# An attention and two-MLP kernel on one core: the first block's output matmul in plain fp32, and the short block moved to the end

## The chip, the core and the metric

One core of a Trainium2 chip. The metric is the device time of one launch in microseconds (us). Engines: PE (matrix multiply; PEld is its weight load), DVE (vector), ACT (scalar, activation functions), POOL (GpSimd), SP (issues the DMAs here).

## The reference, cut to what matters

With `q`, `k`, `v` of 6016 tokens x 256 channels:

```
qn, kn = q / (norm over tokens + 1e-6), k / (norm over tokens + 1e-6)
x  = v @ softmax(kn.T @ qn / tau)                     # 256 x 256 attention over channels
h  = x @ w_in                                         # 6016 x 2048
g  = (a0 + a1 h + a2 h^2 + a3 h^3) / (1 + |b0| |h| + |b1| h^2 + 1e-6)
x2 = g @ w_out                                        # 6016 x 256      (MLP 1)
h  = x2 @ w_in2
g  = h * clip(h + 3, 0, 6) / 6
out = g @ w_out2                                      # 6016 x 256      (MLP 2)
```

The four weights come as float64 (4 MB each) and are turned into fp32 on the chip, a quarter ("group" 0 to 3, 1 MB) at a time.

## The kernel before, in words

**Stages.** First q and k stream in, in 14 chunks of 1, 2, ten times 4, 3 and 1 rows per partition. PE multiplies them in fp32 (L250), ACT squares them (L240), DVE adds the squares (L242). Then come the norms (L281 to L304), the softmax (L319 to L327), and `w1` = attention times `w_in` (`W0a` ... `W3`, L339), so that MLP 1 is `v @ w1`. Its result is split into a high and a low part (`E..h` on ACT, `E..l` on DVE, L349 and L351).

**Split matmuls.** A plain fp32 matmul takes several passes in the array. So the MLP's operands are split: high part (fp32r) and low part (the rest, fp32r). A product is then high x high, low x high (weights) and high x low: 6 passes for each of two output halves, 12 fp32r matmuls with N = tokens of the block. One such set of 12 is called an M below.

**Blocks and steps.** `BLOCKS = [384] + [512] * 11` tokens. A step does 256 of the 2048 hidden channels of a block, so a block has 8 steps and there are 96, with MLP 2 running 10 steps behind MLP 1. In a step s: `M1` (input matmul, L374), `U1` = |b1 h| and `P1` on ACT; `DS`, `P2`, `P3` on DVE; `AB`, `LN`, `EX` on ACT, which make 1/Q as exp(-ln Q). For step s-1: `HI` (high part of g), `N2` and `DD` on DVE, `LO` (low part of g) on DVE or, as `LOP`, on POOL. `M3` is the output matmul of step s-2 (L379, into `y`). MLP 2: `M2` (L374), `C1` (ACT), `C2` (DVE), `H2` (ACT), `L2` or `L2P` (DVE or POOL), `M4` (L379, into `o`). `Vh`, `Vl`, `Yh`, `Yl` split the inputs of the MLPs.

**Weight conversion.** `conv(name, group, part)`: `s` and `b` on ACT, `j` on DVE (the fp32 weight), `h` on ACT (its high part), `l` on DVE or `p` on POOL (its low part).

**Order.** Each engine runs its queue in order. For steps 0 to 21 the order of all engines is the hand-made list `FILL`; after that `ORDER` repeats per step. `chain` ties the instructions of each engine to that order. `shares` remembers the last DVE instruction that reads two SBUF tiles, and `behind` makes a POOL instruction wait for it.

**Tiles.** Working tiles of 128 x 1024 fp32 come from pools by tag: `U` 3, `P` 3, `B` 2, `C` 2, `hi` 3, `lo` 3, `vo` 1. The q and k chunks use `hi`, `U`, `lo`, `P`, so a chunk's load waits until an earlier chunk is done with its tile.

Of the kernel before, what the change touches and what calls it, by code (L numbers as in the profile page):

```python
# [18 lines left out]
BLOCKS = [384] + [512] * 11  # L19
# [42 lines left out]
def attention_rational_relu6_kernel(ctx: ExitStack, tc, q, k, vT, tau, w_in, w_out, ca, cb, w_in2, w_out2, outT):  # L62
# [139 lines left out]

# [56 lines left out]
    nc.sync.dma_start(out=col[:, 0:4], in_=ca.partition_broadcast(128))
    load_w("wi1", 1)
    load_v(0)
    load_w("wi1", 2)
    load_w("wi1", 3)
    for name in ("wo1", "wi2"):  # L270
        for g in range(4):
            load_w(name, g)
# [3 lines left out]
    nc.vector.reciprocal(out=rt, in_=TAU)
    s2k, s2q = tails
    for i in range(4):
        a, t = ((acc_k, s2k), (acc_q, s2q))[i // 2]
        h = slice((i % 2) * 128, (i % 2) * 128 + 128)  # L280
        nc.tensor.matmul(ssp[:, 0, i:i + 1], a[:, h], ones[:, 0:1], start=True, stop=False)  # L281
        nc.tensor.matmul(ssp[:, 0, i:i + 1], t[:, h], ones[:, 0:1], start=False, stop=True)
# [16 lines left out]
    for c in range(2):
        nc.vector.tensor_scalar(out=diag[:, c * 128:(c + 1) * 128], in0=ident, scalar1=inv[:, 2 + c:3 + c], scalar2=None, op0=ALU.mult)  # L300

    nc.vector.tensor_scalar(out=inv[:, 0:2], in0=inv[:, 0:2], scalar1=rt, scalar2=-1.0, op0=ALU.mult, op1=ALU.mult)
    products(LAST - 1)
    nc.tensor.matmul(ssp[:, 1, 0:256], ones, diag, start=True, stop=True)  # L304
    products(LAST)
    for p in "sbj":
        conv("wi1", 1, p)
    split_v(0, "h")
    split_v(0, "l")
# [326 lines left out]
```

## Time and profile before

| | |
|---|---|
| time, 3 runs | 1145.67 us median (1145.56 to 1145.82) |
| span of the profiled execution (first to last instruction) | 1141.5 us; its time around the span is not recorded, the median lies 4.2 us above it |
| PE busy | 1100.4 us, 96% |
| DVE busy | 1009.6 us, 88% |
| ACT busy | 819.8 us, 72% |
| POOL busy | 251.6 us, 22% |

```profile
PE   8986689999999999999999999999999999999998
DVE  6689999988999999998998998998998999999954
ACT  6798986776776777777677676786776776776643
PEclk9998899999999999999999999999999999999999
DMA  9980000000010010010010010010010010000000
```

Each digit is a slice of 28.5 us, in tenths of its length; PEclk is the granted TensorE clock in tenths of full speed.

### The profile page before, as it was taken

What the parts mean: (1) busy time and instruction counts of PE and PEld (TensorE: products, weight loads), DVE (VectorE), ACT (ScalarE), POOL (GpSimd) and SP (SyncE); (2) the same over time, 40 slices, a digit from 0 to 9 for tenths busy, and PEclk for the clock granted to TensorE, in tenths of its full rate; (3) what the DMA queues carried; (4) which work ended last, traced back from release to release, by engine and by line L of the source; (5) the groups of instructions that cost most, each with busy time, mean ns of one, the idle gap of its engine ahead of it and who ended that gap; (6) DMA issues with size and microseconds to landing.
All of it is one profiled execution on the core that took longest, in us unless ns stands there. A gap on an engine that the chain in (4) does not pass through costs nothing.

```text
span 1141.5 us, 12312 instructions
## 1 busy us (share of the span) xinstructions
PE 1100.4 (96%) x4870; PEld 914.1 (80%) x4870; DVE 1009.6 (88%) x872; ACT 819.8 (72%) x802; POOL 251.6 (22%) x115
## 2 busy tenths in 40 slices
PE   8986689999999999999999999999999999999998
PEld 7756578877888888888888888888888888888887
DVE  6689999988999999998998998998998999999954
ACT  6798986776776777777677676786776776776643
POOL 0013335222221222212212222122122221221200
PEclk9998899999999999999999999999999999999999
DMA  9980000000010010010010010010010010000000
GB/s 358 369 327 1 19 1 1 15 19 1 1 37 1 1 38 1 1 37 1 1 37 1 1 38 1 1 37 1 1 37 1 1 37 1 1 19 1 1 19 18
DMA packets 17464, 42.20 MB, mean 37 GB/s; under 512 B 1536, under 2 KB 2560, under 8 KB 17408
## 3 DMA queue, kind: packets, MB, share of 16 engines
q1 hardware_dynamic: 17408, 41.43, 9.9%
q8 instruction: 38, 0.62, 0.2%
q14 instruction: 18, 0.15, 0.0%
HBM read 35.26 MB, written 6.16 MB: 36 GB/s over the span
## 4 chain that ended last, share of the span: by engine, by line
PE 86%; DVE 6%; ACT 4%; issue 2%; DMA 1%; POOL 0%; SPq 0%; POOLq 0%; DVEq 0%; ACTq 0%
PE h L374 41%; PE y L379 21%; PE o L379 20%; PE y L250 3%; DVE B L421 1%; ACT P L406 1%; DVE P L430 1%; DVE P L416 1%; ACT U L411 1%; DVE hi L544 1%; DVE P L556 1%; DMA lo<-in_q_dram 1%; DVE B L550 1%; ACT U L434 0%; DVE q L160 0%
## 5 line engine op out<-in xcount | busy, mean ns | idle before, releaser
L485 POOL TENSOR_TENSOR lo<-C,hi 128x1024 fp32r<-128x1024 f32 (+1 forms) x82 | 195.4, 2383 | 680.5 <-DVE lo L561 649.6
L411 ACT ACTIVATE U<-h,col 128x1024 f32<-128x1024 f32 (+1 forms) x96 | 105.7, 1101 | 180.2 <-PE h L374 179.6
L374 PE MATMUL h<-vh,w 128*128 128x512 f32 (+1 forms) x768 | 194.7, 397 | 20.0 <-DVE P L430 18.8
L379 PE MATMUL y<-hi,wo 128*128 128x512 f32 (+1 forms) x800 | 198.7, 385 | 0.4 <-DVE hi L544 0.4
L374 PEld LDWEIGHTS h<-vh,w 128*128 128x128 f32 x768 | 147.9, 195 | 52.7 <-issue 21.5
L374 PE MATMUL h<-yh,wi 128*128 128x512 f32 (+1 forms) x768 | 187.1, 385 | 3.0 <-DVE C L474 1.8
L379 PE MATMUL o<-hi,wo 128*128 128x512 f32 (+1 forms) x736 | 182.6, 384 | 0.0
L421 DVE SCALAR_TENSOR_TENSOR B<-U,aB,h 128x1024 f32<-128x1024 f32 (+1 forms) x96 | 120.6, 1256 | 61.8 <-ACT P L406 61.6
L379 PEld LDWEIGHTS y<-hi,wo 128*128 128x128 f32 x800 | 149.3, 188 | 29.2 <-DVE hi L544 0.7
L374 PEld LDWEIGHTS h<-yh,wi 128*128 128x128 f32 x768 | 143.2, 188 | 32.3 <-DVE C L474 3.2
L379 PEld LDWEIGHTS o<-hi,wo 128*128 128x128 f32 x736 | 137.6, 188 | 26.6
L469 ACT ACTIVATE C<-h,imm 128x1024 f32<-128x1024 f32 (+1 forms) x96 | 105.1, 1095 | 62.6 <-PE h L374 60.0
L474 DVE SCALAR_TENSOR_TENSOR C<-C,h 128x1024 f32<-128x1024 f32 (+1 forms) x96 | 114.0, 1187 | 16.1 <-ACT C L469 16.1
L544 DVE SCALAR_TENSOR_TENSOR hi<-P,col,U 128x1024 fp32r<-128x1024 f32 (+1 forms) x96 | 125.3, 1306 | 1.0 <-ACT U L438 0.9
L430 DVE SCALAR_TENSOR_TENSOR P<-P,col,h 128x1024 f32<-128x1024 f32 (+1 forms) x96 | 120.7, 1257 | 3.9 <-ACT U L411 1.2
L556 DVE SCALAR_TENSOR_TENSOR P<-P,col,B 128x1024 f32<-128x1024 f32 (+1 forms) x96 | 121.0, 1261 | 2.7
L406 ACT ACTIVATE P<-h,col 128x1024 f32<-128x1024 f32 (+1 forms) x96 | 113.3, 1181 | 6.9 <-PE h L374 5.1
L550 DVE SCALAR_TENSOR_TENSOR B<-B,hi 128x1024 f32<-128x1024 f32 (+1 forms) x96 | 115.8, 1207 | 2.7
L416 DVE TENSOR_TENSOR P<-P,h 128x1024 f32<-128x1024 f32 (+1 forms) x96 | 114.5, 1193 | 3.4 <-ACT U L411 1.9
L480 ACT ACTIVATE hi<-C 128x1024 fp32r<-128x1024 f32 (+1 forms) x96 | 99.6, 1037 | 23.8 <-DVE C L474 21.8
L379 PE MATMUL y<-lo,wo 128*128 128x512 f32 (+1 forms) x400 | 108.3, 388 | 7.6 <-POOL lo L561 7.6
L434 ACT ACTIVATE U<-B,imm 128x1024 f32<-128x1024 f32 (+1 forms) x96 | 108.9, 1134 | 2.7
(101 smaller groups left out, 1296.6 us busy)
## 6 DMA issues: line engine op xcount, KB each, us to landing
raw_wi<-in_moe_w_in_dram SPq DMA_DIRECT2D x8, 1024.0 KB, 13.4
raw_wo<-in_moe_w_out_dram SPq DMA_DIRECT2D x8, 1024.0 KB, 15.1
vo<-in_v_dram SPq DMA_DIRECT2D x11, 512.0 KB, 3.7
out_dram<-vo SPq DMA_DIRECT2D x10, 512.0 KB, 2.8
hi<-in_k_dram SPq DMA_DIRECT2D x5, 512.0 KB, 9.4
lo<-in_q_dram SPq DMA_DIRECT2D x5, 512.0 KB, 10.2
U<-in_k_dram SPq DMA_DIRECT2D x5, 512.0 KB, 10.1
P<-in_q_dram SPq DMA_DIRECT2D x5, 512.0 KB, 10.2
```

The lines of the kernel that those rows point to most:

```text
L374: nc.tensor.matmul(h[j], w_in_at(name, a, c, f + j), x[b][:, c, :], start=(i == 0), stop=(i == 5))
L379: nc.tensor.matmul(y[d], w_out_at(name, a, 2 * pr + j, d), g[b][j], start=(pr == 0 and i == 0), stop=(pr == 7 and i == 5))
L406: nc.scalar.activation(out=halves(c["P"], T), in_=c["h"], func=AF.Identity, scale=A3, bias=A2)
L411: nc.scalar.activation(out=halves(c["U"], T), in_=c["h"], func=AF.Abs, scale=B1)
L416: nc.vector.tensor_tensor(out=p, in0=p, in1=c["h"], op=ALU.mult)
L421: nc.vector.scalar_tensor_tensor(out=halves(c["B"], T), in0=halves(c["U"], T), scalar=aB0, in1=c["h"], op0=ALU.add, op1=ALU.mult)
L430: nc.vector.scalar_tensor_tensor(out=p, in0=p, scalar=A1, in1=c["h"], op0=ALU.add, op1=ALU.mult)
L474: nc.vector.scalar_tensor_tensor(out=x, in0=x, scalar=6.0, in1=h, op0=ALU.min, op1=ALU.mult)
L485: i2 = e.tensor_tensor(out=x, in0=y, in1=z.bitcast(F32), op=ALU.subtract)
L544: shares(nc.vector.scalar_tensor_tensor(out=c["Hi"][:, fa], in0=P[:, fa], scalar=A0, in1=U[:, fa], op0=ALU.add, op1=ALU.mult))
L550: shares(nc.vector.scalar_tensor_tensor(out=B[:, fa], in0=B[:, fa], scalar=ONE_EPS, in1=c["Hi"][:, fa].bitcast(F32), op0=ALU.add, op1=ALU. ...
L556: shares(nc.vector.scalar_tensor_tensor(out=P[:, fa], in0=P[:, fa], scalar=A0, in1=B[:, fa], op0=ALU.add, op1=ALU.subtract))
```

## The change

- `BLOCKS` becomes `[512] * 11 + [384]`.
- For steps 0 to 7 of MLP 1 (now a block of 512 tokens) g is kept as one fp32 tile. `m_out` then does 4 fp32 matmuls with the unsplit fp32 weight (`single`) in place of 12 fp32r ones. `LO` is gone in these steps. P is made with negated coefficients, and `DD` becomes `hi = (B - 2) * hi`.
- In the same steps the denominator comes from r = |h| sqrt|b1|: `U1` uses sqrt|b1|, `DS` is `(U + |b0| / sqrt|b1|) * U` (U only, no longer `h`), `AB` adds the constant 1 + 1e-6, `LN` has no bias, and `N2` is a plain product `B * U` that no longer reads `HI`'s result. It may run on POOL (`N2P`). The small values for that are made once (`nB`, `nN`, `nR`, `nS`, `nQ`).
- The fp32 weight of `wo1` lies in a `lo` tile until its group's `h` and `p` parts and the first block's `M3` are done.
- `LOP` now goes through `behind`; the tiles of `LO`, `L2`, `Vl`, `Yl` are allocated where they are written.
- The list now also orders the q and k phase, with a load item for each DMA (`lk`, `lq`, `lw`, `lv`, `ls`); one group of `w_in2` is loaded and converted (`s`, `b`, `j`, `h`) among the q and k chunks.

```
-BLOCKS = [384] + [512] * 11
+BLOCKS = [512] * 11 + [384]
+F3 = R1 = QX = frozenset(range(8))        # F2, F4 are empty
...
     def m_out(y, name, g, pr, T, split=False):
+        if len(g) == 1:
+            for j, d in ((j, d) for j in range(2) for d in range(2)):
+                o = 256 * ((2 * pr + j) % 4) + 128 * d
+                nc.tensor.matmul(y[d], single[name, pr // 2][:, o:o + 128], g[0][j],
+                                 start=(pr == 0 and j == 0), stop=(pr == 7 and j == 1))
+            return
...
             def DS():
+                if s in R1:
+                    shares(nc.vector.scalar_tensor_tensor(out=c["B"][:, f], in0=c["U"][:, f], scalar=CB, in1=c["U"][:, f],
+                                                          op0=ALU.add, op1=ALU.mult))
+                    return
...
+            def n2(e):
+                U, B, P = operands()
+                x = U[:, fa] if one else c["Hi"][:, fa].bitcast(F32)
+                if a in QX:
+                    i = e.tensor_tensor(out=B[:, fa], in0=B[:, fa], in1=x, op=ALU.mult)
...
+                (shares if e is nc.vector or a not in QX else behind)(i)
...
+                if one:
+                    hi = c["Hi"][:, fa]
+                    shares(nc.vector.scalar_tensor_tensor(out=hi, in0=B[:, fa], scalar=2.0, in1=hi, op0=ALU.subtract, op1=ALU.mult))
+                    hl1[a] = [halves(c["Hi"], Ta)]
...
+            elif name == "wo1" and F3:
+                f = wk.tile([128, 1024], I32, tag="lo", name="f", bufs=BUFS["lo"])
```

Two pieces of the new list, from the q and k phase and from the norms and softmax:

```
lk0 lq1 lq0 lq2 lk1 lk2 ... lk13 ... lq3 ... lk3 ... lk4 ... lq4 ... lk5 x2 lk6 ... lq5 ... lwi22 lq6 lq9 ... lq7 ... lk7 ... lq8 x5 lq12
nM wi1:0s n0 lv0 x12 nN n1 n2 wi1:0b wo1:2b lwi13 nD wi1:0j nC x13 lwo11 zm0 zm1 Vh ze0 zt0 ze1 wo1:2s zc0 zt1 nQ wi2:2p zc1 wi1:3b W0a
```

What the two lists hold between the starts of M1 (wide: 1024 elements per partition, 512 tokens; narrow: 768 elements, 384 tokens; `w1` evictions: `E` items of 512 and of 256 columns; fp32: `M3` of the first block, or a `W` item):

| from, to | list | DVE wide + conversion | DVE narrow | DVE evictions | PE sets wide, narrow, fp32 | POOL | ACT |
|---|---|---|---|---|---|---|---|
| M1@0, M1@4 | before | 0 + 2 | 19 | 5, 2 | 0, 6, 2 | 3 | 33 |
| | after | 15 + 4 | 0 | 6, 2 | 4, 0, 3 | 3 | 26 |
| M1@4, M1@10 | before | 6 + 9 | 30 | 0 | 2, 9, 0 | 7 | 46 |
| | after | 28 + 1 | 0 | 0 | 6, 0, 5 | 4 | 32 |
| M1@10, M1@16 | before | 43 + 4 | 11 | 0 | 12, 14, 0 | 11 | 56 |
| | after | 56 + 6 | 0 | 0 | 23, 0, 2 | 14 | 68 |
| M1@16, M1@21 | before | 37 + 0 | 2 | 0 | 16, 3, 0 | 6 | 35 |
| | after | 37 + 1 | 0 | 0 | 20, 0, 0 | 10 | 36 |

After `M1@21` itself the list of before holds no further M, that of after one (`M4@20`); otherwise both end with the same sets done.

## Rows read from the trace of the kernel before

**Rows 1.** Busy time by engine, clock and DMA, in stretches of 50 us
```profile
core 0: us, PE busy (x) PEld busy (x) DVE busy (x) ACT busy (x) POOL busy (x), PEclk, DMA share, GB/s
0.00:50.00 50.00, 47.12 (x218) 40.93 (x218) 35.29 (x43) 32.97 (x39) 2.70 (x11) 1.00 0.95 360
...
100.00:150.00 50.00, 33.52 (x140) 29.47 (x140) 49.05 (x47) 47.11 (x50) 19.65 (x9) 0.84 0.04 11
...
500.00:550.00 50.00, 50.00 (x223) 41.40 (x222) 44.46 (x38) 35.30 (x33) 12.04 (x5) 1.00 0.07 22
```

**Rows 2.** The same view between the starts of M1@0, @4, @10, @16, @21 and the end
```profile
59.88:89.02 29.14, 21.33 (x90) 15.70 (x89) 23.78 (x29) 26.84 (x34) 6.03 (x3) 0.99 0.74 282
89.02:136.34 47.32, 31.10 (x133) 28.28 (x133) 45.25 (x46) 43.41 (x48) 15.51 (x7) 0.82 0.04 11
136.34:207.00 70.66, 65.83 (x313) 57.08 (x313) 67.53 (x59) 56.95 (x58) 28.43 (x12) 0.98 0.00 1
207.00:259.80 52.80, 50.79 (x228) 42.11 (x229) 47.55 (x40) 34.68 (x35) 13.37 (x6) 1.00 0.05 18
259.80:1141.50 881.70, 876.77 (x3864) 725.12 (x3864) 783.41 (x646) 616.62 (x581) 185.56 (x77) 1.00 0.04 12
```

**Rows 3.** PE's waits, 0 to 180 us: total us, times, longest
```profile
PE h L374 <- DVE P L430: 16.2, 5, 7.3
PE y L379 <- POOL lo L561: 7.4, 3, 4.2
```

**Rows 4.** Timeline of PE: start us, us, instruction
```profile
30.57 3.62 PE L250 MATMUL y<-lo,hi 128*128 128x256 f32 x16
34.02 3.62 PE L250 MATMUL y<-P,U 128*128 128x256 f32 x16
...
71.96 3.60 PE L339 MATMUL o<-raw_wi,hi 128*128 128x512 f32 x8
...
174.57 1.55 PE L379 MATMUL o<-hi,wo 128*128 128x384 f32 x8
...
176.65 2.01 PE L374 MATMUL h<-vh,w 128*128 128x512 f32 x8
...
1053.37 1.98 PE L374 MATMUL h<-vh,w 128*128 128x512 f32 x8
...
1056.09 1.98 PE L374 MATMUL h<-yh,wi 128*128 128x512 f32 x8
```

**Rows 5.** Timeline of DVE: first row of a gapless run, and the one after it
```profile
84.89 1.01 DVE L556 SCALAR_TENSOR_TENSOR P<-P,col,B 128x768 f32<-128x768 f32 x1
...
87.67 0.74 DVE L351 SCALAR_TENSOR_TENSOR w<-o,small,w 128x512 fp32r<-128x512 f32 x1
...
188.25 1.28 DVE L544 SCALAR_TENSOR_TENSOR hi<-P,col,U 128x1024 fp32r<-128x1024 f32 x1
...
196.54 0.94 DVE L474 SCALAR_TENSOR_TENSOR C<-C,h 128x768 f32<-128x768 f32 x1
```

**Rows 6.** Timeline of DVE, norms and softmax (in brackets: idle before, and its releaser)
```profile
42.81 0.16 DVE L289 TENSOR_SCALAR small<-o 128x4 f32<-128x4 f32 x1
...
50.32 0.48 DVE L319 SCALAR_TENSOR_TENSOR yl<-y,small,yh 128x256 f32<-128x256 f32 x1 [2.60 <-ACT yh L310]
...
53.51 0.42 DVE L325 COPY hi<-h 128x256 f32<-128x256 f32 x1 [0.59 <-PE h L324]
```

**Rows 7.** Busy time, clock and DMA of 30 to 40 us (columns of Rows 1)
```profile
30.00:40.00 10.00, 10.00 (x48) 8.81 (x47) 9.56 (x12) 7.16 (x9) 0.00 (x0) 1.00 0.87 316
```

**Rows 8.** Timeline of POOL and DVE, side by side
```profile
137.48 1.84 POOL L561 TENSOR_TENSOR lo<-P,U 128x768 fp32r<-128x768 f32 x1
137.49 2.92 DVE L544 SCALAR_TENSOR_TENSOR hi<-P,col,U 128x1024 fp32r<-128x1024 f32 x1
```

**Rows 9.** Groups by form, 59.88 to 259.8 us: count, busy us, mean ns, idle before
```profile
L544 DVE SCALAR_TENSOR_TENSOR hi<-P,col,U 128x1024 fp32r<-128x1024 f32 x12 | 18.7, 1561 | 1.0 <-ACT U L438 0.9
...
L171 POOL TENSOR_TENSOR wi<-q,wi 128x1024 fp32r<-128x1024 f32 x4 | 9.6, 2397 | 5.0 <-ACT P L406 5.0
```

More of the change, by code (lines that the diff above doesn't have):

```diff
@@ L31 @@
 FILL = (
[23 rows of a table removed]
[27 rows of a table added]
 )
 ONE_EPS = 1.0 + 1e-6
+F3 = frozenset(range(8))
+F4 = frozenset()
+F2 = frozenset()
+R1 = frozenset(range(8))
+QX = frozenset(range(8))
 ET = mybir.EngineType
@@ L265, in attention_rational_relu6_kernel @@
[L265 to L272, printed above, removed]
-    rt = small[:, 0:1]
[L276 to L282, printed above, removed]
@@ L283, in attention_rational_relu6_kernel @@
-    for p in "sbj":
-        conv("wi1", 0, p)
-    products(NORM_AT + 1)
+        parts_done.append(i)
+    rt = small[:, 0:1]
     aB0 = const.tile([128, 1], F32, name="aB0")
-    nc.scalar.activation(out=aB0, in_=B0, func=AF.Abs)
+    neg = const.tile([128, 4], F32, name="neg")
+    rbc = const.tile([128, 4], F32, name="rbc")
+    N0, N1, N2_, N3 = (neg[:, i:i + 1] for i in range(4))
+    RB, CB = rbc[:, 0:1], rbc[:, 1:2]
     ss, ln, y0, iy, nrm, inv = (small[:, 4 * j:4 * j + 4] for j in range(1, 7))
-    nc.vector.tensor_scalar(out=ss, in0=ssp[:, 0, 0:4], scalar1=1e-30, scalar2=None, op0=ALU.max)
@@ L299, in attention_rational_relu6_kernel @@
[L299 to L309, printed above, removed]
-    nc.scalar.activation(out=qb, in_=ssp[:, 1, 0:256], func=AF.Copy)
@@ new lines, in softmax @@
+    def softmax(part, c):
+        h, sc = half[c], late["sc"]
+        if part == "m":
+            nc.vector.scalar_tensor_tensor(out=sc[:, h], in0=sp[:, c, 0:256], scalar=inv[:, c:c + 1], in1=late["qb"], op0=ALU.mult, op1=ALU.mult)
+            nc.vector.tensor_reduce(out=nmax[:, c:c + 1], in_=sc[:, h], axis=AX.X, op=ALU.min)
+        elif part == "e":
+            nc.scalar.activation(out=sc[:, h], in_=sc[:, h], func=AF.Exp, scale=-1.0, bias=nmax[:, c:c + 1], accum_out=sm[:, c:c + 1])
+        elif part == "t":
+            if not ep:
+                ep.append(ptile("h1"))
+            for d in range(2):
+                nc.tensor.transpose(ep[0][:, c, d * 128:(d + 1) * 128], sc[:, c * 256 + d * 128:c * 256 + (d + 1) * 128], ident)
+        elif part == "c":
+            if len(ep) == 1:
+                ep.append(halves(wtile("hi"), 256))
+            nc.vector.tensor_copy(out=ep[1][:, :, c * 128:(c + 1) * 128], in_=ep[0][:, c, 0:256].rearrange("p (d t) -> p d t", d=2))
+        else:
+            nc.vector.tensor_scalar(out=rs, in0=sm, scalar1=1e-9, scalar2=None, op0=ALU.add)
+            nc.vector.reciprocal(out=rs, in_=rs)
@@ L330, in attention_rational_relu6_kernel, with load_small @@
+    def load_small(x):
+        if x == "t":
+            nc.sync.dma_start(out=TAU, in_=tau.partition_broadcast(128))
+        elif x == "b":
+            nc.sync.dma_start(out=col[:, 4:6], in_=cb.partition_broadcast(128))
+        else:
+            nc.sync.dma_start(out=col[:, 0:4], in_=ca.partition_broadcast(128))
     w1_ps = {}
@@ L371, in m_in @@
     def m_in(h, name, x, f, T, split=False):
+        if len(x) == 1:
+            for c, j in ((c, j) for c in range(2) for j in range(2)):
+                o = 512 * c + 128 * ((f + j) % 4)
+                nc.tensor.matmul(h[j], single[name, f // 4][:, o:o + 128], x[0][:, c, :], start=(c == 0), stop=(c == 1))
+            return
         for i, j in order(split):
@@ L410, in U1 @@
                 c["U"] = wtile("U")
[L411 removed]
+                nc.scalar.activation(out=halves(c["U"], T), in_=c["h"], func=AF.Abs, scale=RB if s in R1 else B1)
             @add
@@ L424, in AB @@
             def AB():
-                nc.scalar.activation(out=c["B"][:, f], in_=c["B"][:, f], func=AF.Abs)
+                if s in QX:
+                    nc.scalar.activation(out=c["B"][:, f], in_=c["B"][:, f], func=AF.Identity, bias=C_ONE)
+                else:
+                    nc.scalar.activation(out=c["B"][:, f], in_=c["B"][:, f], func=AF.Abs)
+            if s in R1 and s not in QX:
+                ops.pop("AB")
             @add
@@ L487, in l2, with C2 @@
                     (shares if e is nc.vector else behind)(i2)
-            ops["L2"] = lambda: l2(nc.vector)
-            ops["L2P"] = lambda: l2(nc.gpsimd if a is not None else nc.vector)
+            if k2 in F4:
+                ops.pop("H2")
+                first2 = ops["C2"]
+                @add
+                def C2():
+                    first2()
+                    hl2[k2] = [[c["C"][0][:, j, :] for j in range(2)]]
+            else:
+                ops["L2"] = lambda: l2(nc.vector)
+                ops["L2P"] = lambda: l2(nc.gpsimd if a is not None else nc.vector)
         m = s - DELTA
@@ L504, in Yh, with Yl @@
                     c["y"] = yp.pop(y)[:, :, 0:T]
-                    y_hl[y] = [halves(wtile(t, F32R), T) for t in ("yh", "yl")]
+                    y_hl[y] = [halves(wtile("yh", F32 if y in F2 else F32R), T)]
                     nc.scalar.activation(out=y_hl[y][0], in_=c["y"], func=AF.Copy)
-                @add
-                def Yl(y=m // 8):
-                    yh, yl = y_hl[y]
-                    nc.vector.tensor_tensor(out=yl, in0=c["y"], in1=yh.bitcast(F32), op=ALU.subtract)
+                if m // 8 not in F2:
+                    @add
+                    def Yl(y=m // 8):
+                        y_hl[y].append(halves(wtile("yl", F32R), blocks[y][1]))
+                        yh, yl = y_hl[y]
+                        nc.vector.tensor_tensor(out=yl, in0=c["y"], in1=yh.bitcast(F32), op=ALU.subtract)
         m = k2 - 1
@@ L537, in instructions, with operands @@
             fa = slice(0, 2 * Ta)
+            one = a in F3
+            def operands():
+                if a in pend:
+                    c["pend"] = [x[t] for x in [pend.pop(a)] for t in "UBP"]
+                return c["pend"]
             @add
             def HI():
-                first = pend.pop(a)
-                U, B, P = c["pend"] = first["U"], first["B"], first["P"]
-                c["Hi"], c["Lo"] = wtile("hi", F32R), wtile("lo", F32R)
-                shares(nc.vector.scalar_tensor_tensor(out=c["Hi"][:, fa], in0=P[:, fa], scalar=A0, in1=U[:, fa], op0=ALU.add, op1=ALU.mult))
@@ L545, in HI @@
-                hl1[a] = [halves(c[t], Ta) for t in ("Hi", "Lo")]
-            @add
-            def N2():
-                U, B, P = c["pend"]
-                shares(nc.vector.scalar_tensor_tensor(out=B[:, fa], in0=B[:, fa], scalar=ONE_EPS, in1=c["Hi"][:, fa].bitcast(F32),
-                                                      op0=ALU.add, op1=ALU.mult))
+                U, B, P = operands()
+                c["Hi"] = wtile("hi", F32 if one else F32R)
+                shares(nc.vector.scalar_tensor_tensor(out=c["Hi"][:, fa], in0=P[:, fa], scalar=N0 if one else A0, in1=U[:, fa],
+                                                      op0=ALU.add, op1=ALU.mult))
@@ L559, in lo @@
             def lo(e):
-                U, B, P = c["pend"]
+                U, B, P = operands()
+                c["Lo"] = wtile("lo", F32R)
+                hl1[a] = [halves(c[t], Ta) for t in ("Hi", "Lo")]
                 i = e.tensor_tensor(out=c["Lo"][:, fa], in0=P[:, fa], in1=U[:, fa], op=ALU.mult)
-                if e is nc.vector:
-                    shares(i)
-            ops["LO"] = lambda: lo(nc.vector)
-            ops["LOP"] = lambda: lo(nc.gpsimd)
+                (shares if e is nc.vector else behind)(i)
@@ L568, in instructions @@
+            if not one:
+                ops["LO"] = lambda: lo(nc.vector)
+                ops["LOP"] = lambda: lo(nc.gpsimd)
         return ops
@@ L576, in do @@
             steps[at].pop(n)()
-            for same in (("LO", "LOP"), ("L2", "L2P")):
+            for same in (("LO", "LOP"), ("L2", "L2P"), ("N2", "N2P")):
                 if n in same:
@@ L586, in fill @@
             do(n, int(at))
-            if n == "M1" and int(at) % 8 == 4:
-                load_v(int(at) // 8 + 1)
+        elif n[0] == "l":
+            if n[1] in "kq":
+                load_chunk(n[1], int(n[2:]))
+            elif n[1] == "v":
+                load_v(int(n[2:]))
+            elif n[1] == "w":
+                load_w(n[1:4], int(n[4]))
+            else:
+                load_small(n[2])
+        elif n[0] == "s":
+            square(n[1], int(n[2:]))
+        elif n[0] == "a":
+            add_square(n[1], int(n[2:]))
+        elif n[0] == "f":
+            fold(n[1], int(n[2:]))
+        elif n[0] == "x":
+            products(int(n[1:]))
+        elif n[0] == "n":
+            norm(n[1])
+        elif n[0] == "z":
+            softmax(n[1], int(n[2]))
         elif ":" in n:
```

162 lines of the change are left out of this document (92 added, 70 removed), and 50 rows, old and new, of the table FILL.

## The prediction

> **What bounds the kernel now.** I read the busy times by stretch first, then PE's waits, then the timelines. In the middle PE is the bound: 50.00 of 50 us busy, with DVE at 44.46 [rows 1]; from M1@21 on, 876.77 of 881.70 us [rows 2]. So there each PE set costs its full length, and nothing else counts. The first 260 us are different. While q and k come in, PE is busy 47.12 of 50 us [rows 1]: a chunk of four rows starts 3.45 us after the one before (34.02 - 30.57) [rows 4]. Between M1@0 and M1@10 PE is idle for 7.8 of 29.1 and 16.2 of 47.3 us; DVE is busy 45.25 of 47.3, ACT 43.41 [rows 2]. Up to 180 us PE's longest waits are for `P3` on DVE, which frees the h tile (16.2 us), and for the low part from POOL (7.4 us) [rows 3]. DVE also fills 67.53 of 70.66 us up to M1@16; in the last stretch before M1@21 PE leads again (50.79 of 52.80) [rows 2]. The time is thus when M1@21 starts, plus the PE work behind it.
>
> **Prices.** One set of 12 fp32r matmuls is 2.72 us at 512 tokens (1056.09 - 1053.37) and 2.08 at 384 (176.65 - 174.57) [rows 4]. A set of 4 fp32 matmuls with N = 512 is in the trace as a `W` item: 3.60 us to the end of its last record, so 3.45 from start to start, which the q-k chunk with the same columns shows too [rows 4]. A wide DVE instruction is 1.18 us in a gapless run ((196.54 - 188.25) / 7), a narrow one 0.93 ((87.67 - 84.89) / 3), an eviction of 512 columns 0.74 [rows 5], of 256 about 0.5 by that. A POOL instruction is 2.4 us [rows 9].
>
> **The end.** Before, the 32 narrow sets (8 each of M1 to M4) all lie ahead of M1@21; now they lie behind it, where PE has no gaps. That takes 32 x 0.64 = 20.5 us off the stretch behind M1@21. The list of after leaves one more set (M4@20) behind M1@21: +2.7. DVE and ACT shrink with the narrow block too, so PE should stay the bound. From M1@21 to the end: 881.7 - 20.5 + 2.7 = 863.9 us.
>
> **The q and k phase.** The same loads and products, in another order. Two things can hurt. One group of `w_in2` (1 MB) now goes ahead of q chunk 6 on SP's queue, and several loads behind it wait on SP for tiles that an earlier chunk frees (`lq7` for chunk 3, `lq12` for chunk 4). PE takes 1 MB in 3.45 us, which is 300 GB/s, and the loads run at 316 GB/s at 30 to 40 us with their engines 87% busy [rows 7] and at 360 on average [rows 1], so the loads are ahead of PE by then and 1 MB more (2.8 us at 360) fits into their lead. If that cover is missing, up to 2.8 us come on top; from below, PE's whole idle time in the first 50 us is 2.9 us [rows 1], so no more than that is to be gained. The norm items come one chunk later, but the end of the products sets the softmax as before: DVE waited 2.60 us there, until 50.32 [rows 6]. `nQ` puts six small instructions (0.16 us each [rows 6], about 1.1 us together) into the softmax, of which a wait of 0.59 [rows 6] takes half. I take M1@0 at 60.0 (59.88 before) and keep 58 to 63.
>
> **M1@0 to M1@4.** DVE before: 19 x 0.93 + 2 x 1.18 + 5 x 0.74 + 1.0 = 24.7 us in 29.14; ACT, with 33 instructions and 26.84 us, was the fuller one at 92% [rows 2]. After: ACT has 26, and DVE 19 x 1.18 + 6 x 0.74 + 1.0 = 27.9, the largest sum. At the same 92%: 30.3 us.
>
> **M1@4 to M1@10.** Here the new form pays. A step's DVE work was six or seven narrow instructions, about 5.6 us or more, and is now five wide ones, 5.9 us: `LO` is gone and `N2` is on POOL in seven of the eight steps. Conversion falls from 9 DVE items to 1, since low parts of `wo1` aren't needed yet and some groups were converted earlier. Before: 30 x 0.93 + 15 x 1.18 = 45.6 us in 47.32, 96.4%. After: 29 x 1.18 = 34.2, at 96.4% 35.5 us. PE must do 6 x 2.72 + 5 x 3.45 = 33.6 us in it, so the fp32 sets use up PE's former idle time and cost nothing on top as long as the clock holds. The granted clock was 0.82 in this stretch, with PE at 66% [rows 2]; at 93% busy in the next one it was 0.98. If it stays at 0.82, PE needs 33.6 / 0.82 = 41 us, 5.5 more than I take.
>
> **M1@10 to M1@16.** The postponed conversions and two fp32 sets fall here. Before: 47 x 1.18 + 11 x 0.93 = 65.7 us of DVE in 70.66, 93.0%. After: 62 x 1.18 = 73.2, at 93.0% 78.7 us; PE needs 23 x 2.72 + 2 x 3.45 = 69.5.
>
> **M1@16 to M1@21.** PE before: 16 x 2.72 + 3 x 2.08 = 49.8 us in 52.8, 94.3%. After: 20 x 2.72 = 54.4, so 57.7 us; DVE has 38 x 1.18 = 44.8.
>
> **Sum.** M1@21 at 60.0 + 30.3 + 35.5 + 78.7 + 57.7 = 262.2 us (259.8 before), the end at 262.2 + 863.9 = 1126.1 us of span, against 1141.5. With the 4.2 us between span and median: 1130 us. Put otherwise: the start takes in 128 more tokens of all four sets and 2.4 us more time, and the end gives back 20.5.
>
> **N2 on POOL, and DS on U alone.** The trace has no product B * U on POOL. The nearest row, a subtraction of the same size, takes 2.4 us [rows 9], and `DD` must wait for it, but `P2` and `P3` of other steps stand between them in the list. What POOL costs DVE is bounded by two rows. `HI` at 137.49 us took 2.92 us beside a POOL instruction that began 0.01 us earlier, 1.64 more than its 1.28 [rows 5, 8]. All 12 wide `HI` of the start average 1.56 [rows 9], 3.4 us too much in all, beside 27 POOL instructions: 0.13 each. The 31 POOL instructions of after thus cost between 4 and 51 us; I take the low end, since it is the sum over many, and it is already in the shares of 92 to 96%.
>
> The Trainium skill (SBUF - State Buffer, section "SBUF: two separate sides") says that DVE and GpSimd share one pair of ports as an exclusive lock: an instruction of DVE with two SBUF inputs and one of GpSimd that reads SBUF do not overlap, and the loser blocks for the whole instruction. The row at 137.49 agrees (2.92 = 1.84 - 0.01 + about 1.1), and by that rule the new `DS`, which reads U twice in place of U and the PSUM tile h, becomes one more instruction that can be blocked.
>
> **Rivals.**
>
> *The start fills up.* The new order could keep DVE and PE both nearly full, as no stretch of before did. The sums M1@0 to M1@21 are 180.1 us for DVE and 178.7 for PE. At 97% of DVE: 186 us, M1@21 at 246, the end at 1110, the time 1114 us. For it: PE at 100% with DVE at 89% is what the middle shows [rows 1]. Against it: three engines within 6% of each other leave no room for waits. Chance 0.16.
>
> *The start eats the gain.* The fp32 weights of `wo1` occupy `lo` tiles: of three, two are held until after M1@12 and one until after M1@15, so all low parts of both MLPs pass through one tile, then two. Each is then written only when an M3 or M4 has read the one before. A wait of PE for a low part was up to 4.2 us [rows 3]; three of those, 12.6 us, give 1143 us. For it: the list has LOP and L2 in strict turn there. Against it: PE is not the bound in that stretch. Chance 0.12.
>
> *Slower.* POOL and DVE collide. If half of the 31 POOL instructions block a DVE instruction by the full 1.64 us, 25 us come on top: 1155 us. It decides from M1@21 at 277.6 on (259.8 + 17.8), 15.4 us later than I take, that is from nine or ten full collisions. For it: the row at 137.49 [rows 8], and a `DS` that now reads SBUF only. Against it: the mean of 0.13 us. Chance 0.12.
>
> **How the numbers follow.** The forecast of 1130 has 0.60, with a range of its own of 1119 to 1139 (M1@0 from 58 to 63, the clock's 5.5 us, shares two points either way: 4 us). What a measurement of this kernel can tell from no change is about 0.2%, 2.3 us. Faster by more than that (under 1143.4): 0.60 + 0.16 + 0.08 of the second rival = 0.84; the same: 0.04; slower: 0.12. The range of 1113 to 1144 leaves out the slower rival and a part of the first one.
>
> **What would show it.** M1@0 at 60 and M1@4, @10, @16, @21 near 90, 126, 205 and 262; 3.45 us for an M3 of the first block; no PE gaps behind M1@21, where the last block's sets take 2.08. Wrong would be a middle that no longer has PE at 100%, M1@10 later than 136 (then the fp32 form did not unload DVE), or DVE instructions far above 1.3 us beside `N2P`.

## The result and the profile after

The changed kernel takes 1119.05 us (median of 4 runs, 1117.95 to 1119.91), the kernel before 1145.74 beside it: a ratio of 0.9768, 95% interval 0.9754 to 0.9782. 1130 us with a range of 1113 to 1144 was forecast. The profiled execution took 1119.91 us, 1.9 of it around its span of 1118.0.

The page of the kernel after, busy time in 40 slices of 28 us:

```profile
PE   8999899999999999999999999999999999999998
DVE  4899999988998998999999998998999899898854
ACT  5899988866777676776777677676777767677634
PEclk9999999999999999999999999999999999999999
```

The two 6s of PE in slices four and five of before are gone, and the 8s of the clock row. The stretches between M1@0, @4, @10, @16, @21 and the end, columns as in [rows 2]:

```profile
64.08:88.81 24.73, 22.33 (x74) 13.38 (x72) 24.51 (x25) 23.86 (x27) 4.78 (x2) 1.00 0.73 263
88.81:127.34 38.53, 36.18 (x112) 21.85 (x113) 37.15 (x33) 36.60 (x36) 14.30 (x6) 0.96 0.05 15
127.34:200.63 73.29, 70.35 (x293) 54.60 (x293) 71.98 (x61) 67.47 (x66) 31.11 (x13) 1.00 0.00 1
200.63:255.10 54.47, 54.47 (x241) 44.90 (x240) 50.55 (x41) 37.31 (x37) 23.50 (x10) 1.00 0.06 20
255.10:1118.00 862.90, 859.63 (x3877) 722.21 (x3875) 763.34 (x646) 604.30 (x582) 188.28 (x79) 1.00 0.04 12
```

Beside [rows 2]: the last stretch is 18.8 us shorter (881.70 to 862.90), and M1@21 starts 4.7 us earlier (259.80 to 255.10) although eight steps ahead of it are a third wider. Up to M1@16 DVE is busy for 24.51 of 24.73, 37.15 of 38.53 and 71.98 of 73.29 us; in the fourth stretch PE has no gap at all. PE's longest waits between 64 and 300 us, which answer to [rows 3]:

```profile
PE h L392 <- DVE P L465: 3.1, 3, 2.1
PE h L392 <- DVE w L364: 1.7, 2, 1.1
...
PE y L403 <- POOL lo L628: 0.9, 1, 0.9
```

16.2 us of waiting for `P3` have become 3.1, and 7.4 us for a low part 0.9. In the middle PE stays full:

```profile
500.00:550.00 50.00, 50.00 (x223) 41.39 (x222) 45.45 (x38) 36.15 (x34) 10.90 (x5) 1.00 0.03 10
```

### The profile page after: what moved, and what is told of

Same layout as the page of the kernel before. It is cut to its first block, busy times and chain, and to the rows that moved or that the text cites. A ratio compares the mean times of both kernels' runs of the same rounds, so it can differ in the third digit from the quotient of the medians.

```text
span 1118.0 us, 12249 instructions
## 1 busy us (share of the span) xinstructions
PE 1100.9 (98%) x4838; PEld 904.9 (81%) x4838; DVE 990.0 (89%) x866; ACT 816.5 (73%) x805; POOL 267.0 (24%) x121
## 4 chain that ended last, share of the span: by engine, by line
PE 90%; ACT 4%; DVE 3%; DMA 1%; issue 1%; SPq 0%; POOL 0%; DVEq 0%; POOLq 0%
PE h L392 43%; PE o L403 22%; PE y L403 21%; PE y L251 2%; DMA raw_wi<-in_moe_w_in_dram 1%; DMA U<-in_k_dram 1%; ACT q L155 1%; ACT U L436 0%; ACT U L473 0%; ACT P L431 0%; ACT U L469 0%; DVE hi L618 0%; DVE P L441 0%; DVE P L465 0%; DVE w L364 0%
## 5 line engine op out<-in xcount | busy, mean ns | idle before, releaser
L521 POOL TENSOR_TENSOR lo<-C,hi 128x1024 fp32r<-128x1024 f32 x82 | 197.4, 2408 | 634.7 <-DVE lo L628 628.6
L403 PE MATMUL y<-hi,wo 128*128 128x512 f32 (+1 forms) x736 | 180.8, 382 | 0.0
L450 DVE SCALAR_TENSOR_TENSOR B<-U,aB,h 128x1024 f32<-128x1024 f32 (+1 forms) x88 | 110.4, 1254 | 60.5 <-ACT P L431 57.3
L403 PEld LDWEIGHTS y<-hi,wo 128*128 128x128 f32 x736 | 137.6, 188 | 25.5
L621 DVE SCALAR_TENSOR_TENSOR P<-P,col,B 128x1024 f32<-128x1024 f32 (+1 forms) x88 | 110.9, 1261 | 3.0
L597 DVE SCALAR_TENSOR_TENSOR hi<-P,col,U 128x1024 fp32r<-128x1024 f32 (+1 forms) x88 | 111.3, 1265 | 2.6 <-PE y L403 1.1
L465 DVE SCALAR_TENSOR_TENSOR P<-P,col,h 128x1024 f32<-128x1024 f32 (+1 forms) x88 | 110.6, 1256 | 2.9
L431 ACT ACTIVATE P<-h,col 128x1024 f32<-128x1024 f32 (+1 forms) x88 | 103.8, 1180 | 2.9 <-PE h L392 2.7
L392 PE MATMUL h<-vl,w 128*128 128x512 f32 (+1 forms) x384 | 101.3, 385 | 1.0 <-DVE vl L209 1.0
L473 ACT ACTIVATE U<-U 128x1024 f32<-128x1024 f32 (+1 forms) x96 | 100.1, 1043 | 2.4
```

What stands on the lines that cost most here:

```text
L392: nc.tensor.matmul(h[j], w_in_at(name, a, c, f + j), x[b][:, c, :], start=(i == 0), stop=(i == 5))
L403: nc.tensor.matmul(y[d], w_out_at(name, a, 2 * pr + j, d), g[b][j], start=(pr == 0 and i == 0), stop=(pr == 7 and i == 5))
L431: nc.scalar.activation(out=halves(c["P"], T), in_=c["h"], func=AF.Identity, scale=a3, bias=a2)
L450: nc.vector.scalar_tensor_tensor(out=halves(c["B"], T), in0=halves(c["U"], T), scalar=aB0, in1=c["h"], op0=ALU.add, op1=ALU.mult)
L465: nc.vector.scalar_tensor_tensor(out=p, in0=p, scalar=N1 if s in F3 else A1, in1=c["h"], op0=ALU.add, op1=ALU.mult)
L521: i2 = e.tensor_tensor(out=x, in0=y, in1=z.bitcast(F32), op=ALU.subtract)
```

## The experiments

The reading so far had a start that DVE bounds, and a move (the short block) that pays behind M1@21. But three things changed at once: the form of eight steps, the order, and the block that is short. The runs take them apart. All runs but e2 are built on the changed kernel's code, so `behind` on `LOP` and the later allocation of tiles are in all of those; what these two are worth was not run on its own. M1@0 to M1@21 is called the start below.

### The short block alone

In the new kernel, and in the kernel before:

```
-BLOCKS = [512] * 11 + [384]      # e1: changed kernel, 384 first
+BLOCKS = [384] + [512] * 11
```
```
-BLOCKS = [384] + [512] * 11      # e2: kernel before, 384 last, nothing else
+BLOCKS = [512] * 11 + [384]
```

> The changed kernel with the 384-token block first again, list and fp32 form kept. Theory (the end pays back the whole length of 32 matrix sets, the start is bounded by DVE): 32 x 0.64 = 20.5 us more behind M1@21; ahead of it 56 DVE instructions of the first block become narrow, 56 x 0.25 = 14 us less: 1119.1 + 6.5 = 1125.5 us. Rival A (PE is the bound of the start too): both sides 20.5, 1119 us. Rival B (the start waits on chains, not on an engine's sum): start unchanged, 1139 us.

> The kernel before, with the 384-token block last and nothing else. Theory: 20.5 us less behind M1@21, 62 DVE instructions wide instead of narrow ahead of it, 62 x 0.25 = 15.5 us more: 1145.7 - 5 = 1140.7 us. Rival A (the move is the whole change, the start has room): 1125 us. Rival B (waits grow in the old order): 1146 us or more.

Measured (in brackets the ratio to the kernel before and its 95% interval): e1 1126.62 us (0.9833, 0.9815 to 0.9852), so the move gains 7.5 us in the new kernel, close to e1's theory. e2 1148.21 us (1.0019, 1.0007 to 1.003): in the kernel before it gains nothing and loses a little, against e2's theory and as its rival B had it. The stretch of e1 from M1@21 to the end:

```profile
244.20:1126.60 882.40, 878.85 (x3877) 727.21 (x3875) 784.04 (x646) 617.45 (x582) 188.32 (x79) 1.00 0.04 12
```

882.40 against 862.90: the short block behind M1@21 gives back 19.5 us (20.5 predicted), and the same in e2, whose rest is 862.2. What differs is its price ahead of M1@21. The start of e2:

```profile
60.56:282.69 222.13, 191.58 (x763) 149.65 (x761) 204.22 (x172) 174.87 (x172) 68.79 (x27) 0.93 0.13 45
```

222.13 us against 199.92 in the kernel before (29.14 + 47.32 + 70.66 + 52.80 [rows 2]): 22.2 us, more than comes back. DVE's busy time rose from 184.11 (the same four rows) to 204.22 us, 20.1 where the theory had 15.5, and its share stayed at 92%. The start of e1:

```profile
65.17:244.20 179.03, 165.93 (x718) 132.13 (x717) 171.72 (x157) 152.79 (x163) 68.09 (x31) 0.98 0.12 42
```

In the new kernel the same 128 tokens cost 191.0 - 179.0 = 12.0 us.

### Form and order, one without the other

e3 keeps the new order of steps and loads and goes back to the old form of the first eight steps: split result, 12 fp32r matmuls, old denominator, `N2` on DVE behind `HI`, `LOP` after `DD`, and the `h` and `p` parts of `wo1` right behind `j`, since the split form needs them early. e7 has the new form in the order of the kernel before, with `N2P` on POOL where `N2` stood and without `LO` in the eight steps. e11 is e7 with `N2` on DVE.

```
-F3 = R1 = QX = frozenset(range(8))          # e3, on the changed kernel
+F3 = R1 = QX = frozenset()
-... HI@2 P2@2 N2P@2 ... DD@2 ...  wo1:0j E0bl1
+... HI@2 P2@2 N2@2 ... DD@2 LOP@2 ...  wo1:0j wo1:0h wo1:0p E0bl1
```
```
-HI@1 P1@2 P3@1 LN@1 N2@1 U1@2 ... LO@1      # e7: FILL of before, LO dropped
+HI@1 P1@2 P3@1 LN@1 N2P@1 U1@2 ...          # e11: N2@1 again
```

> The changed kernel with the split form in the first 8 steps: 12 fp32r matmuls per M3, LO on POOL, N2 on DVE behind HI, the denominator of before, wo1's high and low parts right behind its fp32 part; the list is otherwise that of the change. Theory: seven N2 come back to DVE, 7 x 1.18 = 8.3 us, PE loses 8 x 0.7 us that were hidden: 1127 us. Rival A (the order alone made the gain): 1119 to 1121 us. Rival B (the form made it): 1138 us or more.

> The changed kernel with the order of before (q and k phase as before, list as before without LO of the first 8 steps, seven N2 on POOL as in the change), short block last. Theory: against the kernel before with the short block last it takes seven N2 and one LO off DVE, 8 x 1.18 = 9.4 us: 1131 us. Rival A (the form does nothing without the new order): 1140 us. Rival B (the order does nothing): 1119 to 1121 us.

> The new code (fp32 result, new denominator, short block last) in the order of the kernel before, as in the earlier run that took 1149.7 us, but with N2 of the seven steps back on DVE. There DVE waited 10.5 us in DD for N2P, which stands right ahead of it in the old order, PE 8.8 us for the high part behind it, and N2P itself waited for DVE. Theory (in the old order the wait of DVE and PE for the POOL step is the loss): 7 products more on DVE cost 7 x 1.18 = 8.3 us, the wait of 10.5 us and most of PE's 8.8 go, so the time falls by 2 to 10 us, to 1140 to 1148. Rival A (the loss is in the old order of ACT and of the conversions, which the new form does not fit): the price of 8.3 us is paid and little comes back, 1153 to 1158. Rival B (N2P is the whole loss of the old order): 1132 or less, as the new list with N2 on DVE took 1129.

Measured: e3 1145.24 us (0.9996, 0.9986 to 1.0005), e7 1149.73 (1.0035, 1.0021 to 1.005), e11 1144.06 (0.9989, 0.9979 to 0.9999). The theories of e3 and e7 missed by 18 and 19 us: against the kernel before, neither the order nor the form gains anything alone. Against e2, which has the short block last as they do, the order gains 3.0 us (e3) and the form 4.1 (e11), both together 29.1; as e2 lacks `behind` on `LOP` and the later tiles, the 3.0 and the 4.1 can in part be theirs. e11's theory held: by the ratios (0.9989 against 1.0035) the POOL step is a loss of some 5 us in the old order. DVE's waits in the start of e7, total us, times, longest:

```profile
DVE hi L618 <- POOL B L604: 10.5, 5, 2.3
DVE P L441 <- ACT U L436: 5.9, 5, 1.5
DVE B L450 <- ACT P L431: 5.2, 5, 1.8
```

The first is `DD`, which the old order puts right behind `N2P`. In e11 that wait is gone and DVE works 7.3 us more instead. In e3 it is the U and P tiles that come free late. PE's longest wait in its start, and two of ACT's:

```profile
PE h L393 <- DVE P L466: 18.9, 6, 6.0
```
```profile
ACT U L437 <- POOL lo L629: 10.7, 3, 4.9
...
ACT P L432 <- POOL lo L629: 6.0, 2, 4.1
```

`LOP` of a split step reads U and P and takes 2.6 us on average in e3's start, behind other POOL work; ACT's next `U1` and `P1` wait 16.7 us for it. The fp32 form has no such step, and in the changed kernel's start ACT's only wait for POOL is 1.8 us (for a tile of MLP 2).

### The parts of the form in the new order

```
-HI@1 N2P@1 P3@1 ...                         # e5: N2 on DVE in all eight steps
+HI@1 N2@1 P3@1 ...
```
```
-R1 = QX = frozenset(range(8))               # e10: e5, and the old denominator
+R1 = QX = frozenset()
```
```
-wo1:0j E0bl1 ...                            # e9: h and p of wo1 right behind j,
+wo1:0j wo1:0h wo1:0p E0bl1 ...              # all else as changed
```

> The changed kernel with the seven N2P back on DVE, in their places of the list. Theory (DVE's sum bounds the first ten steps): 7 x 1.18 = 8.3 us more of DVE where it is 61.6 of 63.2 us busy: 1126 to 1127 us. Rival A (what POOL takes over it gives back by blocking DVE and by its 1.2 us longer step in the chain): 1119 to 1121 us.

> The changed kernel with the denominator of before in the first 8 steps (DS reads h, AB is the absolute value, LN has the bias, N2 is the fused instruction on DVE); g in one fp32 tile and the fp32 M3 are kept. Theory: as many instructions per engine as with N2 on DVE, so the same 1126 to 1127 us. Rival A (DS on h holds the h tile longer and PE waits for it): 1131 us or more.

> The changed kernel with wo1's high and low parts made right behind its fp32 part, as the split form would need them, instead of being put off; fp32 form kept. Theory (sums): four h on ACT, 4.2 us, where ACT is 60.5 of 63.2 us busy, and four POOL instructions; little is given back, as DVE bounds the next stretch: 1121 to 1123 us. Rival A (putting them off is most of the gain, by waits of POOL and lo tiles): 1129 us or more. Rival B (no matter): 1119 us.

Measured: e5 1128.95 us (0.985, 0.9832 to 0.9869), 9.9 more than the changed kernel, where its theory had 7 to 8 and its rival A at most 2: in this order what POOL takes over is gain. e10 1131.08 (0.9869, 0.9851 to 0.9887): the denominator alone is worth 2.1. The two intervals overlap, as each holds the spread of the kernel before, but the four executions of e10 (1130.88 to 1131.70) all lie above those of e5 (1128.51 to 1129.62). It is what e10's rival A had; PE's waits for `P3` are 12.1 us in its start, 9.8 in e5's and 3.1 in the changed kernel's, which is in line with its reason without proving it. e9 1126.50 (0.9827, 0.9806 to 0.9849), 7.5 more, between its two expectations: the late high and low parts of `wo1` matter, by less than the whole form. So, in the new order, N2 on POOL gives 9.9 us, the denominator 2.1 and the rest (fp32 result and late parts of `wo1`) 1145.24 - 1131.08 = 14.2.

The starts of six kernels that all have the short block last, one row each, tell why the parts don't add up. After the length come the engines; DVE is the third.

The kernel before with the block moved (e2) stands above. New form, old order, `N2` on DVE (e11):

```profile
62.17:280.11 217.94, 191.23 (x730) 139.31 (x729) 198.29 (x171) 174.32 (x172) 47.85 (x20) 0.95 0.12 43
```

New form, old order, `N2` on POOL (e7):

```profile
61.47:285.10 223.63, 191.32 (x731) 139.45 (x729) 190.96 (x164) 174.49 (x172) 67.99 (x27) 0.95 0.12 42
```

Old form, new order (e3):

```profile
63.91:280.28 216.37, 185.51 (x751) 145.66 (x749) 202.29 (x165) 167.27 (x164) 81.81 (x32) 0.94 0.11 40
```

New form, new order, `N2` on DVE (e5):

```profile
64.66:264.86 200.20, 185.77 (x719) 135.72 (x717) 193.05 (x164) 166.36 (x163) 56.59 (x24) 0.98 0.11 39
```

The changed kernel:

```profile
64.08:255.10 191.02, 183.34 (x718) 134.73 (x717) 184.19 (x157) 165.25 (x163) 73.69 (x31) 0.99 0.12 43
```

| kernel | order | form | N2 | start | DVE instructions | DVE busy | DVE idle | time |
|---|---|---|---|---|---|---|---|---|
| e2 | old | old | DVE | 222.1 | 172 | 204.2 | 17.9 | 1148.2 |
| e11 | old | new | DVE | 217.9 | 171 | 198.3 | 19.7 | 1144.1 |
| e7 | old | new | POOL | 223.6 | 164 | 191.0 | 32.7 | 1149.7 |
| e3 | new | old | DVE | 216.4 | 165 | 202.3 | 14.1 | 1145.2 |
| e5 | new | new | DVE | 200.2 | 164 | 193.1 | 7.2 | 1129.0 |
| after | new | new | POOL | 191.0 | 157 | 184.2 | 6.8 | 1119.1 |

Read DVE's busy and idle columns apart. The form takes 5.9 us of DVE's busy time off in the old order and 9.2 in the new, and N2 on POOL another 7.3 or 8.9. That is much alike in both. The idle time is not: in the old order it grows as DVE's busy time goes, by 1.7 and by 13.0 us; in the new order it falls, by 6.9 and 0.3. In the old order less to do for DVE becomes more waiting for ACT and POOL (the waits of e7 above); in the changed kernel's start none of DVE's waits sums to more than 1.2 us. The two shares of the 31.1 us between e2's start and the changed kernel's are 20.0 us of busy time and 11.1 of waiting.

Busy time is not work alone. The form takes one DVE instruction off (`LO`); the rest of its 5.9 or 9.2 us is instructions that got shorter. And e3 has 7 instructions fewer than e2, but only 1.9 us less busy time: its `N2` average 1506 ns against 1237, its `DD` 1385 against 1280. It has 32 POOL instructions in its start, e2 has 27; that they are the cause was not tested. Which of the moved items make the order fit was not taken apart further.

### The first 64 us

M1@0 came at 64.08 us, 4.2 later than before. The timeline of PE there, before:

```profile
3.71 1.91 PE L250 MATMUL y<-lo,hi 128*128 128x256 f32 x4
6.02 2.26 PE L250 MATMUL y<-P,U 128*128 128x256 f32 x8 [0.39 <-DMA P<-in_q_dram]
9.77 2.40 PE L250 MATMUL y<-lo,hi 128*128 128x256 f32 x10 [1.50 <-DMA lo<-in_q_dram]
...
46.17 2.75 PE L250 MATMUL y<-lo,hi 128*128 128x256 f32 x12
...
53.32 1.97 PE L339 MATMUL h<-raw_wi,hi 128*128 128x256 f32 x8
```

and after:

```profile
4.75 2.04 PE L251 MATMUL y<-lo,hi 128*128 128x256 f32 x4 [0.83 <-DMA lo<-in_q_dram]
8.39 3.66 PE L251 MATMUL y<-P,U 128*128 128x256 f32 x8 [1.59 <-DMA U<-in_k_dram]
11.89 3.62 PE L251 MATMUL y<-lo,hi 128*128 128x256 f32 x16
...
48.12 2.19 PE L251 MATMUL y<-lo,hi 128*128 128x256 f32 x9
...
55.90 3.32 PE L352 MATMUL o<-raw_wi,hi 128*128 128x256 f32 x8
59.02 2.19 PE L352 MATMUL h<-raw_wi,hi 128*128 128x256 f32 x8
```

The new list loads q chunk 0 third and k chunk 1 fifth, the third chunk's products begin 2.1 us later, and from there PE runs on without a gap to x12, 1.95 us late. The softmax starts 2.6 us late (DVE at 52.91, 50.32 before), and then the two halves of `W0` take 5.15 us (55.90 to 61.05) in place of 3.53 (53.32 to 56.85). Two runs tried to mend it:

```
-lk0 lq1 lq0 lq2 lk1 lk2 ... zt1 nQ wi2:2p   # e6
+lk0 lq0 lk1 lq1 lk2 lq2 ... nQ fk512 ... zt1 wi2:2p
```
```
-lwi22 lq6 ... wi2:2b ak4 ... wi2:2s ...     # e8: e6, and the w_in2 group three chunks
+lq6 ... x5 lwi22 lq12 ... x7 wi2:2b ...     # later, its conversions with it; n1 wi1:0s
```

> The changed kernel with the first loads in the order k0 q0 k1 q1 k2 q2 and the six small instructions of nQ ahead of the folds. Theory (the q and k phase lies on the path one for one): the chunk of four rows that started at 11.9 us starts at 9.8 as before, and nQ's 0.6 us leave the softmax: 1119.1 - 2.7 = 1116.4 us. Rival A (the order behind has slack that takes it up): 1119 us.

> The changed kernel with the start rearranged: loads k0, q0, k1, q1, k2, q2 in this order, the group of w_in2 loaded three chunks later (behind q chunk 8 in the list) and its four conversions moved with it, nQ ahead of the load of the short k rows, n1 ahead of the first conversion of w_in. In the earlier run with the loads and nQ alone the products began 1 us earlier, but the chunks x4 to x7 then trailed their loads and the last one ended later than before. Theory (the 1 MB load of w_in2 between the early chunks takes the gain away): with it moved, the last product ends near 46.5 us, the softmax starts near 51.5, M1@0 at 61 to 62 instead of 64.1, and the time falls by about 2.5 us, to 1116 to 1117 us. Rival A (the loads bound the phase wherever the 1 MB lies): M1@0 at 63 to 64 and the time within 1 us of the changed kernel's 1119. Rival B (DVE, which is full from M1@4 on, takes up what an earlier M1@0 gives): M1@0 at 61 to 62, M1@21 no earlier than 254, time 1118 to 1119.

> The changed kernel itself once more, on the same chip as its rearranged form, so that the two are compared on one chip. All theories: 1118 to 1120 us, M1@21 within 1.5 us of 255.1, the stretch behind it 862 to 864.

Measured: e6 1118.15 us (0.9755, 0.9737 to 0.9774), e8 1121.71 (0.9793, 0.9779 to 0.9807), the changed kernel again 1119.09 (0.9766, 0.975 to 0.9783). e6 can't be told from the changed kernel. In its profile the third chunk began at 10.84 us, 1.1 earlier, but PE was then busy for only 9.16 and 9.57 of 10 us from 10 to 30, and x12 began at 48.90, 0.8 later than in the changed kernel. e8 is 2.6 us slower, and its theory falls. PE in e8:

```profile
3.81 2.04 PE L252 MATMUL y<-lo,hi 128*128 128x256 f32 x4
5.65 2.39 PE L252 MATMUL y<-P,U 128*128 128x256 f32 x8
10.70 3.69 PE L252 MATMUL y<-lo,hi 128*128 128x256 f32 x16 [2.67 <-DMA lo<-in_q_dram]
...
42.60 3.62 PE L252 MATMUL y<-P,U 128*128 128x256 f32 x16
48.31 0.35 PE L291 MATMUL o<-ones,accs 128*128 128x1 f32 x2 [2.09 <-DVE accs L246]
```

The products did come earlier, but by 0.4 us at the last full chunk (42.60, 42.97 in the changed kernel), and behind it PE waits 2.09 us for the sums of squares on DVE. The conversions that e8 moved now lie among the last squares and sums (DVE busy for 9.77 us of 40 to 50, 8.36 in the changed kernel). M1@0 is at 65.58 in e8, but at 65.45 in the second profile of the changed kernel too, with the loads as they were: a single profile's M1@0 does not tell what an order of the loads is worth. Nor do the profiles show where e8's 2.6 us arise, as its profiled execution is its fastest (1120.42 us). No version beats the changed kernel.

## Why the prediction was right

**The mechanism** held in outline: the end gives back the narrow sets, the start takes in 128 tokens more and M1@21 still comes 4.7 us earlier than before, and the middle keeps PE at 50.00 of 50 us (500 to 550 us). The forecast was 11 us too high, and 1119.05 lies at the lower edge of its own range (1119 to 1139). Each term can be set beside its stretch:

| term | predicted | measured |
|---|---|---|
| M1@0 | 60.0 | 64.1 |
| M1@0 to M1@4 | 30.3 | 24.7 |
| M1@4 to M1@10 | 35.5 | 38.5 |
| M1@10 to M1@16 | 78.7 | 73.3 |
| M1@16 to M1@21 | 57.7 | 54.5 |
| M1@21 to the end | 863.9 | 862.9 |
| around the span | 4.2 | 1.9 |

The misses of the single stretches, up to 5.6 us and in both directions, cancel in part; to that extent the sum is luck.

**The end** was right to 1.0 us, and no PE wait stands behind M1@21. Its two terms were further off and cancel: the narrow sets gave back 19.5 us, not 20.5 (881.7 to e2's 862.2, neither with `M4@20`), and `M4@20` cost 0.7, not 2.7 (862.2 to 862.9, and 881.7 to e1's 882.4), as PE's idle time in the stretch fell from 4.9 to 3.3 us.

**The shares taken over from before were the wrong step.** I took each stretch of the start at 92 to 96% of its fullest engine, because the stretches of before stood there. Order and form together decide that share, and both changed: 96.4% over the whole start (184.19 of 191.02), 100% of PE in its last stretch. The rival "the start fills up" had this figure (97%), and its 1114 us is nearer to the result than 1130. It overshot mainly because M1@0 came 4.1 us late and DVE was busy for 184.2 us, not 180.1. The split between the stretches is off for a plainer reason: DVE trails the list by a few instructions at each M1 (25 ran from M1@0 to M1@4, not the 27 that the list has there, and 33 in the next, not 29; one that lies across a border counts on both sides).

**N2 on POOL** was called cheap, and the low end of its bounds (4 to 51 us) was taken. The low end held. The groups by form in the changed kernel, start first, then behind M1@21; the figure after the comma is the mean in ns:

```profile
L606 DVE SCALAR_TENSOR_TENSOR B<-B,hi 128x1024 f32<-128x1024 f32 x12 | 17.3, 1439 | 0.1
L450 DVE SCALAR_TENSOR_TENSOR B<-U,aB,h 128x1024 f32<-128x1024 f32 x13 | 16.6, 1276 | 1.3 <-ACT U L436 1.0
L597 DVE SCALAR_TENSOR_TENSOR hi<-P,col,U 128x1024 fp32r<-128x1024 f32 x12 | 16.3, 1360 | 2.6 <-PE y L403 1.1 <-PE o L403 0.9 <-ACT U L473 0.6
L447 DVE SCALAR_TENSOR_TENSOR B<-U,rbc 128x1024 f32<-128x1024 f32 x8 | 10.2, 1281 | 0.2
...
L597 DVE SCALAR_TENSOR_TENSOR hi<-P,col,U 128x1024 fp32r<-128x1024 f32 x68 | 86.9, 1279 | 0.0
L606 DVE SCALAR_TENSOR_TENSOR B<-B,hi 128x1024 f32<-128x1024 f32 x69 | 85.8, 1244 | 2.3
```

The old-form `N2` and `HI` of the start are 0.195 and 0.081 us longer than behind M1@21: 12 x 0.195 + 12 x 0.081 = 3.3 us in all. The rival "slower" needed 15.4. And not even this is the price of `N2P`: in e5, with `N2` on DVE, the same two groups are as long:

```profile
L606 DVE SCALAR_TENSOR_TENSOR B<-B,hi 128x1024 f32<-128x1024 f32 x12 | 17.6, 1467 | 0.1
...
L597 DVE SCALAR_TENSOR_TENSOR hi<-P,col,U 128x1024 fp32r<-128x1024 f32 x12 | 16.3, 1358 | 2.6 <-PE y L403 1.1 <-PE o L403 0.9 <-ACT U L473 0.6
```

The place in the list matters here too. In the changed kernel the seven `N2P` (2386 ns on average) lie beside `P2`, `P3`, a `DS` with h and evictions, which all read a PSUM tile, and beside the first 0.3 us of two `HI`; none of these is more than 0.1 us longer than its kind. The new `DS` that reads U alone (L447) has 1281 ns and the one with h (L450) 1276, so it lost nothing. In the old order `N2P` averages 2881 ns (e7) and this `DS` 1428 (e7) and 1429 (e11). The rule of the Trainium skill that the forecast weighed (SBUF — State Buffer, section "SBUF: two separate sides"), by which the loser blocks for the whole instruction, agrees with the longer means of `N2` and `HI`; `DS`, which it put at risk, escaped in the new order and not in the old.

**M1@4 to M1@10** was 3.0 us over. The granted clock was 0.84 from 89 to 100 us; in the second profile of the changed kernel it was 1.00 from 90 to 100 us and the stretch 37.3, so some 1.2 us of it go with the clock. It did rise from the 0.82 of before, as the forecast had it, and an fp32 `M3` took the 3.60 us that the `W` item had:

```profile
84.23 3.60 PE L398 MATMUL y<-hi,f 128*128 128x512 f32 x8
```

**M1@0** missed its own range of 58 to 63, by two steps. The first is "the same loads and products, in another order", which put the order of the first loads at nothing: the first three chunks are late, and PE, full from 11.89 us on, has nothing to make that up with. "The loads are ahead of PE by then" held in this profile (PE busy for 10.00 of 10 us in each stretch from 10 to 50), but for PE's late start: in e6, which started the third chunk 1.1 us earlier, PE had gaps behind it. How the order and the 1 MB share the 2 us stays open; that the 2.8 us priced for the 1 MB are near the 2.6 measured at the softmax is luck. The second step is the clock, which has no term in the q and k phase: the halves of `W0` took 5.15 us with a granted clock of 0.83 from 50 to 60 us, and 3.53 before and 3.46 in e6, where it was 1.00.

**The time around the span.** The 4.2 us set the profiled span of one execution against the median of others. Other executions of the kernel before have 2.0 to 2.4 (1143.36 with a span of 1141.2), so the profiled one was by this about 2 us shorter than the median. 2 us of the miss are that.

**The other rivals.** "The start eats the gain" (one tile for low parts): 0.9 us of PE waits. That the parts would each carry a share was never questioned in the forecast. The runs of a part alone (e2, e3, e7 and e11, 1144.1 to 1149.7 us) show that this would have been wrong: the forecast came right for the whole by a fit of order and form for which it had no term.

## What to carry to other kernels

When an order written out by hand and a change of form come together, don't price either by the engine's share of before: the share belongs to the pair. Measure the bound engine's busy and idle time apart, and count its instructions, as busy time also holds what made them longer; work taken off an engine is a gain only if the order doesn't turn it into waiting. Moving narrow tiles to where the matrix engine is full pays by their missing columns, but only as far as the place they leave can take wider ones.

## What the runs showed of the hardware that was not expected

The granted clock fell to 0.83 between 50 and 60 us in the changed kernel (0.86 in the second profile), and stayed at 1.00 in e6 and in the kernel before, although PE's two idle times in the softmax are the same in all of them (1.82 and 0.61 us). `W0a`, behind these, took 3.32 us in the one case and 1.89 in e6. In e8 the mean is 0.83 too, but there the clock fell ahead of the softmax, behind PE's wait of 2.09 us: it was 0.50, the lower of its two levels (1.2 and 2.4 GHz), from 52 to 54 us, x12 took 4.52 us in place of 2.84, and `W0a` 1.89. Of the other profiles six have 0.83 to 0.90 in that stretch (e1, e5, e7, e9, e10, e11) and two 1.00 (e2, e3). Executions of the changed kernel with a mean clock of 1.0 over the span took 1116.96 to 1118.30 us, those with 0.997 or 0.998 took 1119.05 to 1120.26: about 2 us that no line of the kernel sets. The Trainium skill (TensorE: Matmul & The Clock Gate, section "Part 1: The HAM clock gate (the "warmup" mystery)") says that the point at which a kernel's matmuls pass from the slow clock to the fast one differs from run to run. These executions of one kernel, at 0.997 to 1.0, agree that the clock is not the same in every run; what the skill tells of is the rise, and here it is the fall that comes or stays away.
